# Outer products, key sums and query products moved from GpSimd to VectorE, batch 1 started behind chunk 0, scratch reads spread over 16 source rows

## The chip, the cores and the metric

The kernel runs on one NeuronCore of a Trainium2 chip. The metric is the device time of one launch in microseconds, as the median of several runs. The engines are named as the profile names them: PE (TensorE, matmuls), DVE (VectorE), ACT (ScalarE), POOL (GpSimd) and SP (SyncE, which here only issues transfers). Each has its own instruction stream, which it works through in program order; they meet at semaphores.

## What is computed

Two stages, everything in float32. First an attention with a polynomial feature map: every row of q and k (4 batches, 4 heads, 1088 rows of 32) is projected by two 8x32 matrices, and the outer product of the two projections gives 64 features. Then a gated feed-forward block runs over the 4352 tokens of 128 values which the attention gives.

```python
def phi(x):
    a = np.einsum('rd,bhsd->bhsr', S1, x)
    b = np.einsum('rd,bhsd->bhsr', S2, x)
    return np.einsum('bhsi,bhsj->bhsij', a, b).reshape(*x.shape[:-1], r * r)
q_p, k_p = (phi(q), phi(k))
kv = np.einsum('bhsf,bhsd->bhfd', k_p, v)
z = np.sum(k_p, axis=2)
num = np.einsum('bhsf,bhfd->bhsd', q_p, kv)
den = np.einsum('bhsf,bhf->bhs', q_p, z)[..., None] + 1e-06
x = (num / den)                       # then (B,H,S,D) -> (B*S, H*D)
gate = 1.0 / (1.0 + np.exp(-(x @ w_gate)))
out = (gate * (x @ w_val)) @ w_out    # 128 -> 1536 -> 128
```

## The kernel before

The feed-forward block is the bulk of the work. The tokens are cut into chunks of 512 (the ninth has 256). For each chunk the 1536 hidden units are worked through in twelve pieces of 128. One such piece is called a wave here: `w1` computes gate and value on PE into a two-bank PSUM tile `wave` (two buffers), ACT makes the sigmoid `sg`, DVE multiplies it with the value into `g` (`glu`, L317), and `w2` multiplies `g` with a slice of `w_out` on PE and accumulates into `moeout` (L256). `glu` of a wave is issued just before `w1` of the next one, and `w2` follows with a lag of two waves, so that PE has something to do while ACT and DVE work. After twelve waves DVE transposes the sum (`o_sb`, L266) and SP stores it.

The order of all instructions on PE, DVE, ACT and POOL is written out by hand: no scheduler moves them. The function `slot(group, waves)` issues one attention step (`group`) and then so many waves; the main program is a list of slots. A wave is only issued when its chunk's tokens exist (`moe["ready"]`).

The weights arrive in a 64-bit form and are narrowed on the chip while chunk 0 runs: `narrow` is a generator of four steps, whose operations are on POOL (`cap` L97, `head` L114), ACT (`tail` L101, `cap` L113) and DVE (`head` L105 and L109, `w_sb` L117). During chunk 0 each wave carries one round of them.

The attention of one batch goes through these steps:

- `turn_k` (L362), `turn_q` (L373): DVE transposes the loaded rows in blocks of 32. `turn_q` takes q in two parts, 8 and 9 blocks wide (`q_chk`); everything about q comes in these two parts, n = 0 and n = 1.
- `begin(b)`: `kps` (L385) projects k on PE, DVE transposes the result to `kab` (L395). `qcomp` (L474) projects q, ACT copies it to `cq`. `spread` (L498, L506) writes `cq` to a scratch in DRAM (`dq`) and reads it back in two arrangements, `qp` and `bq`, so that each of 64 features' two factors is in the right partition. Then `outer` forms the outer products of k, `kp` (L406).
- `sum_z` (L560 to L565): sums `kp` over nine row groups into `zs`.
- `kv` (L526, L538): the product of key features and values, and of the summed features and ones, on PE; ACT copies it to `kvd`.
- `ndt` (L571): PE transposes that; DVE and ACT copy it (`zb`, `nd`).
- `qmult(b, n)` (L515): `qp` times `bq`, the query features.
- `den(b, n)` (L591) and the `invert` that it returns (L602 to L609): the denominator on PE, and its reciprocal on DVE in four operations (`dT`, two on `rc`, `rb`).
- `num(b, n)` (L626) and its `divide` (L636): the numerator on PE and the division on DVE into `xT`, the token matrix.

For batch 0 the outer products are on DVE, and the first query part goes another way (`ab`). Its second part (`q01`) goes through the scratch like the other batches, and `qmult(0, 1)` is on DVE. For batches 1 to 3 `outer`, `sum_z` and `qmult` are on POOL. The main program before reads:

```python
slot(q01, 4)
turn_k(1)
slot(None, 2)
turn_q(1, 0)
turn_q(1, 1)
slot(None, 1)
qmult(0, 1, nc.vector)
slot(lambda: den(0, 1)(), 1)
slot(lambda: num(0, 1)(), 1)
```

and then a loop over batches 1 to 3, in which `turn_k` and `turn_q` of the next batch stand at the end.

Of the kernel before, what the change touches and what calls it, by code (L numbers as in the profile page):

```python
# [8 lines left out]
F32 = mybir.dt.float32  # L9
# [3 lines left out]
ALU = mybir.AluOpType  # L13
ACTF = mybir.ActivationFunctionType
MUL = ALU.mult

P = 128
# [3 lines left out]
def kernel(  # L21
# [12 lines left out]
    nc = tc.nc  # L34

    B, H, S, D = q.shape
    R = S1.shape[0]
    F = R * R
# [7 lines left out]
    NJK = 9  # L46
# [7 lines left out]
    sbA = ctx.enter_context(tc.tile_pool(name="sbA", bufs=2))  # L54
# [302 lines left out]
    def turn_k(b, t0=0, t1=T):  # L357
        if b >= B:
            return
        if t0 == 0:  # L360
            kT_of[b] = sbA.tile([P, T, 32], F32, tag="kT", name="kT", bufs=1)
        nc.vector.transpose(  # L362
            out=kT_of[b][:, t0:t1].rearrange("p t s -> p (t s)"),
            in_=k_t[b][:, t0:t1].rearrange("p t d -> p (t d)"),
        )

    def turn_q(b, n):
        if b >= B:
# [4 lines left out]
        nc.vector.transpose(  # L373
            out=qT_of[b][:, t0 : t0 + tn].rearrange("p t c s -> p (t c s)"),
            in_=q_t[b][:, 2 * t0 : 2 * (t0 + tn)].rearrange("p t d -> p (t d)"),
        )

    KP, QP, BQ, ND, KAB, ASB, KVZ, KVD, RB = {}, {}, {}, {}, {}, {}, {}, {}, {}

    def kps(b):  # L380
        t = ps2.tile([P, 2, 512], F32, tag="two", name="kps")
# [16 lines left out]
        KP[b] = sbA.tile([P, 2, NJK, 2, F], F32, tag="kp", name="kp")  # L398


    def outer(b, pi, m0, m1, j0=0, j1=NJK, eng=nc.gpsimd):
        a0 = KAB[b][:, pi, j0:j1, 2 * R * m0 :]
        pst = list(a0.ap[0])
        jm = [[2 * R, 2 * (j1 - j0)]] if m1 - m0 == 2 else [[4 * R, j1 - j0]]
        o0 = KP[b][:, pi, j0:j1, m0:m1]
        eng.tensor_tensor(  # L406
            out=o0.rearrange("p j m (i l) -> p (j m) i l", i=R),
            in0=bass.AP(tensor=a0.tensor, offset=a0.offset, ap=[pst] + jm + [[1, R], [0, R]]),
            in1=bass.AP(tensor=a0.tensor, offset=a0.offset + R, ap=[pst] + jm + [[0, R], [1, R]]),
            op=MUL,  # L410
        )
# [80 lines left out]
    def spread(b, ns, cq, eng=nc.sync):  # L492
        for n in ns:
            w = 32 * q_chk[n][1]
            d = dram.tile([2, 2, R, H, w], F32, tag=f"dq{n}", name="dq")
            for c in range(2):
                g = 2 * n + c
                eng.dma_start(  # L498
                    out=d[c].rearrange("i r (m p) w -> (i r m) p w", m=2),
                    in_=cq[32 * g : 32 * g + 32, :, :w],  # L500
                )
            for i, t in enumerate((QP[b], BQ[b])):
                for c in range(2):
                    d0 = d[c, i]
                    rows = [[H * w, R], [0, R]] if i == 0 else [[0, R], [H * w, R]]
                    nc.sync.dma_start(  # L506
                        out=half(t, n)[64 * c : 64 * c + 64].rearrange("p h w -> p (h w)"),
                        in_=bass.AP(
                            tensor=d0.tensor, offset=d0.offset, ap=rows + [[1, H * w]]
                        ),  # L510
                    )

    def qmult(b, n, eng=nc.gpsimd):
        q0 = half(QP[b], n)
        eng.tensor_tensor(out=q0, in0=q0, in1=half(BQ[b], n), op=MUL)  # L515

    def kv(b, j_list, zsum=None):

# [34 lines left out]
            ),  # L553
        )

    def sum_z(b):

        kp = KP[b].rearrange("p c j m f -> p c j (m f)")
        z4 = sbA.tile([P, 2, 4, 2 * F], F32, tag="z4", name="z4", bufs=1)
        nc.gpsimd.tensor_tensor(out=z4, in0=kp[:, :, 1:5], in1=kp[:, :, 5:9], op=ALU.add)  # L560
        nc.gpsimd.tensor_tensor(out=z4[:, :, :2], in0=z4[:, :, :2], in1=z4[:, :, 2:], op=ALU.add)
        zs = sbA.tile([P, H, F], F32, tag="zs", name="zs")
        zc = zs.rearrange("p (c m) f -> p c (m f)", c=2)
        nc.gpsimd.tensor_tensor(out=zc, in0=z4[:, :, 0], in1=z4[:, :, 1], op=ALU.add)
        nc.gpsimd.tensor_tensor(out=zc[:64], in0=zc[:64], in1=kp[:64, :, 0], op=ALU.add)  # L565
        return zs

    def ndt(b, pool=(ps1, "one")):
        ndps = pool[0].tile([P, 2, 256], F32, tag=pool[1], name="ndps")
# [77 lines left out]
    for _ in range(3):  # L647
# [9 lines left out]
        out=sk,  # L657
# [4 lines left out]
        op=MUL,  # L662
# [19 lines left out]
    mult10 = ab(None, (0, 1, 0), (psm, "wave"))  # L682
    for j0, j1 in ((0, 5), (5, NJK)):
        for pi in range(2):
            outer(0, pi, 0, 2, j0, j1, nc.vector)
        if j0 == 0:
            kv(0, [1, 2, 3, 4])
    narrow_w(0, 0)
# [21 lines left out]
    cq = {}  # L710

    def begin(b):
        glu()
        kps(b)
        cq[b] = qcomp(b, (0, 1), (psm, "wave"))
        spread(b, (0, 1), cq[b])
        for pi in range(2):
            for m in range(2):
                outer(b, pi, m, m + 1)

    def num0_den1(b):
        divide = num(b, 0)
        invert = den(b, 1)
        divide()
        invert()
# [65 lines left out]
```

## Time and profile before

| what | value |
|---|---|
| time, median of 3 runs | 314.44 us (313.09 to 315.10) |
| profiled execution | 318.37 us, span 316.6 us |
| PE busy | 302.6 us, 96% of the span |
| DVE busy | 137.0 us, 43% |
| ACT busy | 80.7 us, 25% |
| POOL busy | 66.0 us, 21% |
| DMA moved | 22.91 MB, 72 GB/s over the span |
| one wave on PE, L296 and L256 | 1.72 + 0.86 us |
| POOL: `outer` 14.0, `qmult` 14.9, `sum_z` L560 7.2 | us busy in all |

The busy shares tell which engine is full, not what a change is worth. PE is busy nearly all the time, so the time that can be won lies in those few places where it isn't, or where it runs slowly. These are found in the chain of work that ended last (its pieces in order of time show holes between PE's pieces), in the waits of PE, and in the timeline around each hole. The profiled execution is a little longer than the timed ones.

### The profile page before, as it was taken

What the parts mean: (1) busy time and instruction counts of PE and PEld (TensorE: products, weight loads), DVE (VectorE), ACT (ScalarE), POOL (GpSimd) and SP (SyncE); (2) the same over time, 40 slices, a digit from 0 to 9 for tenths busy, and PEclk for the clock granted to TensorE, in tenths of its full rate; (3) what the DMA queues carried; (4) which work ended last, traced back from release to release, by engine and by line L of the source; (5) the groups of instructions that cost most, each with busy time, mean ns of one, the idle gap of its engine ahead of it and who ended that gap; (6) DMA issues with size and microseconds to landing.
All of it is one profiled execution on the core that took longest, in us unless ns stands there. A gap on an engine that the chain in (4) does not pass through costs nothing.

```text
span 316.6 us, 3687 instructions
## 1 busy us (share of the span) xinstructions
PE 302.6 (96%) x1394; PEld 136.4 (43%) x1394; DVE 137.0 (43%) x235; ACT 80.7 (25%) x149; POOL 66.0 (21%) x64
## 2 busy tenths in 40 slices
PE   7889969999799999999999999999999999999995
PEld 2423313454234444443344444443444444444684
DVE  4988986323665221354453213552223223222321
ACT  2535513212113222222122222122222222222230
POOL 1346613951101942100019321000000000000000
PEclk9999968999999999999999999999999999999999
DMA  7996620455204456120005550020002000200021
GB/s 182 351 371 175 175 96 1 114 141 128 46 0 143 111 138 143 36 33 0 2 1 129 124 100 0 1 35 0 0 0 33 0 2 0 33 0 0 0 35 17
DMA packets 28465, 22.91 MB, mean 72 GB/s; under 512 B 19616, under 2 KB 23584, under 8 KB 28448
## 3 DMA queue, kind: packets, MB, share of 16 engines
q1 hardware_dynamic: 27520, 22.14, 27.0%
q10 hardware_dynamic: 928, 0.54, 0.8%
q8 instruction: 11, 0.18, 0.2%
q14 instruction: 6, 0.05, 0.1%
HBM read 19.46 MB, written 3.21 MB: 72 GB/s over the span
## 4 chain that ended last, share of the span: by engine, by line
PE 85%; DVE 8%; DMA 3%; issue 1%; POOL 1%; SPq 0%; ACT 0%; POOLq 0%; DVEq 0%
PE wave L296 52%; PE moeout L256 27%; DMA w_in<-in_moe_w_out_dram 2%; PE dps L591 2%; DMA k<-in_k_dram 1%; DVE w_sb L117 1%; PE nps L626 1%; PE kvz L526 1%; DVE head L105 1%; DVE g L317 1%; DVE rc L604 1%; DVE qp L515 1%; POOL head L114 1%; PE kps L385 1%; DVE head L109 1%
## 5 line engine op out<-in xcount | busy, mean ns | idle before, releaser
L296 PE MATMUL wave<-xT,w_sb 128*128 128x512 f32 (+1 forms) x432 | 192.6, 573 | 1.2 <-DVE w_sb L117 1.2
L317 DVE TENSOR_TENSOR g<-wave,sg 128x512 f32<-128x512 f32 x102 | 70.0, 688 | 143.0 <-ACT sg L304 142.7
L296 PEld LDWEIGHTS wave<-xT,w_sb 128*128 128x128 f32 x432 | 82.2, 191 | 97.2 <-issue 87.6
L304 ACT ACTIVATE sg<-wave 128x512 f32<-128x512 f32 x102 | 60.9, 597 | 212.1 <-PE wave L296 211.2
L256 PE MATMUL moeout<-g,w_sb 128*128 128x512 f32 (+1 forms) x216 | 105.5, 582 | 1.8 <-DVE g L317 1.8
L256 PEld LDWEIGHTS moeout<-g,w_sb 128*128 128x128 f32 x216 | 39.3, 191 | 46.3 <-issue 39.2
L406 POOL TENSOR_TENSOR kp<-kab 128x576 f32<-128x576 f32 x12 | 14.0, 1201 | 60.0 <-DVE kab L395 60.0
L515 POOL TENSOR_TENSOR qp<-qp,bq 128x1024 f32<-128x1024 f32 (+1 forms) x6 | 14.9, 2483 | 31.6 <-DMA bq<-dq 31.6
L114 POOL TENSOR_TENSOR head<-head,tail 128x384 int32<-128x384 int32 (+1 forms) x13 | 13.7, 1054 | 24.3 <-DVE head L109 22.9
L636 DVE TENSOR_TENSOR xT<-nps,rb 128x512 f32<-128x512 f32 (+1 forms) x8 | 5.8, 725 | 14.1 <-PE nps L626 14.0
L591 PE MATMUL dps<-qp,zb 128*32 128x256 f32 (+1 forms) x64 | 5.8, 438 | 3.3 <-DVE qp L515 3.1
L117 DVE SCALAR_TENSOR_TENSOR w_sb<-cap,head 128x384 f32<-128x384 f32 x12 | 8.1, 676 | 0.8 <-POOL head L114 0.8
L97 POOL TENSOR_SCALAR cap<-w_in 128x384 f32<-128x384 f32 x12 | 7.1, 594 | 5.0 <-DMA w_in<-in_moe_w_out_dram 5.0
L109 DVE SCALAR_TENSOR_TENSOR head<-cap,head 128x384 int32<-128x384 int32 (+1 forms) x13 | 7.6, 582 | 0.4
L113 ACT ACTIVATE cap<-cap 128x384 f32<-128x384 f32 (+1 forms) x13 | 6.5, 497 | 4.4 <-DVE head L109 4.4
L229 PE MATMUL warm<-ones 128*128 128x512 f32 (+1 forms) x10 | 6.6, 788 | 1.0 <-DVE hm L235 1.0
L560 POOL TENSOR_TENSOR z<-kp 128x1024 f32<-128x1024 f32 x3 | 7.2, 2406 | 0.2
L101 ACT ACTIVATE tail<-w_in 128x384 int32<-128x384 uint32 x12 | 6.6, 560 | 1.4 <-DMA w_in<-in_moe_w_out_dram 1.4
L626 PE MATMUL nps<-qp,nd 64*32 64x256 f32 (+1 forms) x128 | 6.1, 401 | 0.9 <-issue 0.9
L526 PEld LDWEIGHTS kvz<-kp,v 128*32 128x32 f32 (+1 forms) x288 | 5.3, 109 | 3.3 <-issue 2.7
L266 DVE STREAM_TRANSPOSE o_sb<-moeout 128x512 f32<-128x512 f32 (+1 forms) x9 | 6.1, 679 | 1.4 <-PE moeout L256 1.3
L526 PE MATMUL kvz<-kp,v 128*32 128x64 f32 (+1 forms) x288 | 6.6, 222 | 0.1
(57 smaller groups left out, 88.5 us busy)
## 6 DMA issues: line engine op xcount, KB each, us to landing
v<-in_v_dram SPq DMA_DIRECT2D x16, 144.0 KB
qp<-dq SPq DMA_DIRECT2D x8, 288.0 KB
bq<-dq SPq DMA_DIRECT2D x8, 288.0 KB
k<-in_k_dram SPq DMA_DIRECT2D x3, 544.0 KB
q<-in_q_dram SPq DMA_DIRECT2D x3, 544.0 KB
w_in<-in_moe_w_gate_dram SPq DMA_DIRECT2D x6, 256.0 KB
w_in<-in_moe_w_val_dram SPq DMA_DIRECT2D x6, 256.0 KB
w_in<-in_moe_w_out_dram SPq DMA_DIRECT2D x6, 256.0 KB
```

Source lines behind the costliest of these rows:

```text
L109: nc.vector.scalar_tensor_tensor(out=head, in0=cap, scalar=-0x40000000, in1=head, op0=ALU.bitwise_and, op1=ALU.bitwise_or)
L114: nc.gpsimd.tensor_tensor(out=head, in0=head, in1=tail, op=ALU.add)
L117: nc.vector.scalar_tensor_tensor(out=out, in0=cap.bitcast(F32), scalar=1.265625 * 2.0**-30, in1=head.bitcast(F32), op0=ALU.is_ge, op1=MUL,)
L256: nc.tensor.matmul(out=moe["acc"][:, :tw], lhsT=w_sb[:, 2, j, :], rhs=g[:, jj, :tw], start=(j == 0), stop=(j == NJ - 1),)
L296: nc.tensor.matmul(out=wv[:, which, jj * tw : (jj + 1) * tw], lhsT=w_sb[:, which, j0 + jj, :], rhs=xT[:, t0 : t0 + tw], start=True, stop=True,
L304: nc.scalar.activation(out=sg, in_=wv[:, 0], func=ACTF.Sigmoid)
L317: nc.vector.tensor_tensor(out=g, in0=wv[:, 1], in1=sg, op=MUL)
L406: eng.tensor_tensor(out=o0.rearrange("p j m (i l) -> p (j m) i l", i=R), in0=bass.AP(tensor=a0.tensor, offset=a0.offset, ap=[pst] + jm + [ ...
L515: eng.tensor_tensor(out=q0, in0=q0, in1=half(BQ[b], n), op=MUL)
L526: nc.tensor.matmul(out=kvz[32 * h : 32 * h + 32, F * which : F * which + F], lhsT=v_t[b][:kr, h, j, :] if which == 0 else ones[:kr, :], rh ...
L591: nc.tensor.matmul(out=dps[32 * h : 32 * h + 32, :w], lhsT=zb[b % 2][:, h, :], rhs=half(QP[b], n)[:, 2 * (h % 2) + h // 2, :], start=True, ...
L626: nc.tensor.matmul(out=nps[32 * h : 32 * h + 32, c, :w], lhsT=ND[b][rows, 32 * h : 32 * h + 32], rhs=half(QP[b], n)[rows, 2 * (h % 2) + h ...
```

## The change

Four edits, made together:

1. `outer`, `sum_z` and `qmult` of batches 1 to 3 go from POOL to DVE. `outer` takes both head pairs' halves at once (two operations of 128x1152 for a batch in place of four of 128x576). `sum_z` is cut into two steps, and each piece is put between waves.
2. Batch 1 moves behind chunk 0: its `turn_k` and `turn_q` no longer stand between the waves of chunk 0, `slot(q01, 8)` runs eight waves without them, and each batch is turned at the start of its own round.
3. `spread` writes `cq` in pieces of 16 partitions, four for each part in place of two, with the scratch laid out so that the reading of `qp` is one transfer whose source has 16 rows, each read 8 times, in place of two transfers whose sources have 8 rows each. The reading of `bq` stays two transfers of 8 repeats.
4. The loop over batches has another list of slots: one wave (batch 1) or two waves (batches 2 and 3) after each attention step.

It is meant [...] to bring the second query part of batch 0 forward, and to use more of the transfer engines for the scratch.

```diff
-    def outer(b, pi, m0, m1, j0=0, j1=NJK, eng=nc.gpsimd):
+    def outer(b, pi, j0=0, j1=NJK):
...
-        eng.tensor_tensor(
-            out=o0.rearrange("p j m (i l) -> p (j m) i l", i=R),
...
+        nc.vector.tensor_tensor(
+            out=KP[b][:, pi, j0:j1].rearrange("p j m (i l) -> p (j m) i l", i=R),
...
             for c in range(2):
-                g = 2 * n + c
-                eng.dma_start(
-                    out=d[c].rearrange("i r (m p) w -> (i r m) p w", m=2),
-                    in_=cq[32 * g : 32 * g + 32, :, :w],
+                for i in range(2):
+                    p0 = 64 * n + 32 * c + 16 * i
+                    eng.dma_start(
+                        out=d[i, c].rearrange("r (m p) w -> (r m) p w", m=2),
+                        in_=cq[p0 : p0 + 16, :, :w],
+                    )
+
+            nc.sync.dma_start(
+                out=half(QP[b], n).rearrange("p h w -> p (h w)"),
+                in_=bass.AP(
+                    tensor=d.tensor, offset=d.offset, ap=[[H * w, 2 * R], [0, R], [1, H * w]]
+                ),
+            )
...
-    def qmult(b, n, eng=nc.gpsimd):
+    def qmult(b, n):
         q0 = half(QP[b], n)
-        eng.tensor_tensor(out=q0, in0=q0, in1=half(BQ[b], n), op=MUL)
+        nc.vector.tensor_tensor(out=q0, in0=q0, in1=half(BQ[b], n), op=MUL)
...
-    def sum_z(b):
-
+    def sum_z(b, step):
...
+        def add(out, in0, in1):
+            nc.vector.tensor_tensor(out=out, in0=in0, in1=in1, op=ALU.add)
...
-        for pi in range(2):
-            for m in range(2):
-                outer(b, pi, m, m + 1)
...
-    slot(q01, 4)
-    turn_k(1)
-    slot(None, 2)
-    turn_q(1, 0)
-    turn_q(1, 1)
-    slot(None, 1)
-    qmult(0, 1, nc.vector)
+    slot(q01, 8)
+    qmult(0, 1)
     slot(lambda: den(0, 1)(), 1)
     slot(lambda: num(0, 1)(), 1)
     for b in range(1, B):
         more = b + 1 < B
-        wn = 2 if b == 1 else 3
+        wn = 1 if b == 1 else 2
+        turn_k(b)
+        turn_q(b, 0)
+        slot(None, wn)
+        turn_q(b, 1)
+        slot(lambda: begin(b), 1)
         load_kq(b + 1)
-        slot(lambda: begin(b), wn)
-        zs = sum_z(b)
-        slot(None, 2 * wn - 1)
-        qmult(b, 0)
-        slot(lambda: kv(b, [1, 2, 3, 4, 5, 6, 7, 8, 0], zs), wn)
+        for pi in range(2):
+            outer(b, pi)
+            slot(None, wn)
+        for step in range(2):
+            sum_z(b, step)
+            slot(None, wn)
+        slot(lambda: kv(b, [1, 2, 3, 4, 5, 6, 7, 8, 0], ZS[b]), wn)
         if more:
             v_t[b + 1] = load_v(b + 1)
-        slot(lambda: ndt(b), wn - 1)
+        slot(lambda: ndt(b), wn)
+        qmult(b, 0)
+        slot(lambda: den(b, 0)(), wn)
         qmult(b, 1)
-        slot(lambda: den(b, 0)(), wn)
-        slot(lambda: num0_den1(b), wn)
-        slot(lambda: num(b, 1)(), 1)
-        turn_k(b + 1)
-        slot(None, 1)
-        turn_q(b + 1, 0)
-        turn_q(b + 1, 1)
-        slot(None, 1)
+        slot(lambda: num0_den1(b), wn + 1)
+        slot(lambda: num(b, 1)(), 3)
     slot(None, 10**3)
```

More of the change, by code (lines that the diff above doesn't have):

```diff
@@ L376, in turn_q @@
         )
-    KP, QP, BQ, ND, KAB, ASB, KVZ, KVD, RB = {}, {}, {}, {}, {}, {}, {}, {}, {}
+    KP, QP, BQ, ND, KAB, ASB, KVZ, KVD, RB, Z4, ZS = ({} for _ in range(11))
     def kps(b):
@@ L398, in kps @@
         KP[b] = sbA.tile([P, 2, NJK, 2, F], F32, tag="kp", name="kp")
[L401 to L409 removed]
+    def outer(b, pi, j0=0, j1=NJK):
+        a0 = KAB[b][:, pi, j0:j1]
+        ap = [list(a0.ap[0]), [2 * R, 2 * (j1 - j0)]]
+        nc.vector.tensor_tensor(
+            out=KP[b][:, pi, j0:j1].rearrange("p j m (i l) -> p (j m) i l", i=R),
+            in0=bass.AP(tensor=a0.tensor, offset=a0.offset, ap=ap + [[1, R], [0, R]]),
+            in1=bass.AP(tensor=a0.tensor, offset=a0.offset + R, ap=ap + [[0, R], [1, R]]),
             op=MUL,
@@ L496, in spread @@
             for c in range(2):
-                g = 2 * n + c
-                eng.dma_start(
-                    out=d[c].rearrange("i r (m p) w -> (i r m) p w", m=2),
-                    in_=cq[32 * g : 32 * g + 32, :, :w],
-                )
[L502 to L511, printed above, removed]
-    def qmult(b, n, eng=nc.gpsimd):
+                for i in range(2):
[10 more added lines that the diff above has]
+            )
+            for c in range(2):
+                d0 = d[1, c]
+                nc.sync.dma_start(
+                    out=half(BQ[b], n)[64 * c : 64 * c + 64].rearrange("p h w -> p (h w)"),
+                    in_=bass.AP(
+                        tensor=d0.tensor, offset=d0.offset, ap=[[0, R], [H * w, R], [1, H * w]]
+                    ),
+                )
+    def qmult(b, n):
         q0 = half(QP[b], n)
-        eng.tensor_tensor(out=q0, in0=q0, in1=half(BQ[b], n), op=MUL)
+        nc.vector.tensor_tensor(out=q0, in0=q0, in1=half(BQ[b], n), op=MUL)
     def kv(b, j_list, zsum=None):
@@ L554, in kv @@
         )
-    def sum_z(b):
+    def sum_z(b, step):
         kp = KP[b].rearrange("p c j m f -> p c j (m f)")
[L559 to L566, printed above, removed]
+        def add(out, in0, in1):
+            nc.vector.tensor_tensor(out=out, in0=in0, in1=in1, op=ALU.add)
+        if step == 0:
+            Z4[b] = sbA.tile([P, 2, 4, 2 * F], F32, tag="z4", name="z4", bufs=1)
+            add(Z4[b], kp[:, :, 1:5], kp[:, :, 5:9])
+            return
+        z4 = Z4[b]
+        add(z4[:, :, :2], z4[:, :, :2], z4[:, :, 2:])
+        ZS[b] = sbA.tile([P, H, F], F32, tag="zs", name="zs", bufs=1)
+        zc = ZS[b].rearrange("p (c m) f -> p c (m f)", c=2)
+        add(zc, z4[:, :, 0], z4[:, :, 1])
+        add(zc[:64], zc[:64], kp[:64, :, 0])
     def ndt(b, pool=(ps1, "one")):
@@ L684 @@
         for pi in range(2):
-            outer(0, pi, 0, 2, j0, j1, nc.vector)
+            outer(0, pi, j0, j1)
         if j0 == 0:
```

## The prediction

> **What bounds the kernel now.** I read the busy shares first, then the slices, then PE's waits, then the timeline around the two largest waits, and last the granted clock there.
>
> ```profile
> PE 302.6 (96%) x1394; PEld 136.4 (43%) x1394; DVE 137.0 (43%) x235; ACT 80.7 (25%) x149; POOL 66.0 (21%) x64
> ...
> PE   7889969999799999999999999999999999999995
> ...
> POOL 1346613951101942100019321000000000000000
> PEclk9999968999999999999999999999999999999999
> ```
>
> PE is full. From slice 12 (95 us) on it shows no hole at all, so whatever DVE or POOL do in batches 2 and 3 costs nothing today. The weak slices are the start, slices 5 and 6 (40 to 55 us, low clock with them) and slice 10 (79 to 87 us).
>
> ```profile
> PE dps L591 <- DVE qp L515: 3.1, 1, 3.1
> PE moeout L256 <- DVE g L317: 1.8, 1, 1.8
> PE wave L296 <- DVE w_sb L117: 1.2, 3, 0.6
> ```
>
> PE's waits are few: two single ones and a sum of 1.2 us in chunk 0. The timeline names what made them. First the one at 40 to 43 us:
>
> ```profile
> 37.90 0.60 ACT L304 ACTIVATE sg<-wave 128x512 f32<-128x512 f32 x1 [1.65 <-PE wave L296]
> 38.05 1.36 DVE L373 STREAM_TRANSPOSE qT<-q 128x512 f32<-128x512 f32 x2
> ...
> 39.34 0.65 DVE L317 TENSOR_TENSOR g<-wave,sg 128x512 f32<-128x512 f32 x1
> ...
> 41.02 1.15 POOL L114 TENSOR_TENSOR head<-head,tail 128x384 int32<-128x384 int32 x1 [1.51 <-DVE head L109]
> 41.23 2.15 DVE L515 TENSOR_TENSOR qp<-qp,bq 128x1152 f32<-128x1152 f32 x1
> ...
> 43.44 1.19 PE L591 MATMUL dps<-qp,zb 128*32 128x288 f32 x8 [3.06 <-DVE qp L515]
> ```
>
> `qmult(0, 1)` is late because DVE first does `turn_q(1)`, then the gate product, then three narrowing operations, then itself, at 2.15 us. Next the one at 80 to 82 us:
>
> ```profile
> 77.92 2.62 POOL L515 TENSOR_TENSOR qp<-qp,bq 128x1152 f32<-128x1152 f32 x1 [6.78 <-DMA bq<-dq]
> ...
> 78.18 2.38 DVE L604 TENSOR_SCALAR rc<-dT 128x16 f32<-128x16 f32 x1
> ...
> 82.23 1.12 PE L256 MATMUL moeout<-g,w_sb 128*128 128x512 f32 x2 [1.83 <-DVE g L317]
> ```
>
> The 16-element operation on `rc` took 2.38 us; its 18-element sister takes 0.17 (172 ns mean). It ended at 80.56, and POOL's product ended at 80.54. DVE stood still, the gate products behind it came late, PE waited 1.83 us. The clock during the first wait (columns: stretch, sum, busy of PE, PEld, DVE, ACT, POOL, then clock, DMA share, GB/s):
>
> ```profile
> 41.00:42.00 1.00, 0.00 (x0) 0.00 (x0) 1.00 (x2) 0.93 (x3) 0.98 (x1) 1.00 0.97 379
> 42.00:43.00 1.00, 0.00 (x0) 0.00 (x0) 1.00 (x1) 0.00 (x0) 0.16 (x1) 0.77 0.16 60
> 43.00:44.00 1.00, 0.56 (x8) 0.20 (x8) 0.38 (x1) 0.00 (x0) 0.00 (x0) 0.50 0.00 0
> ...
> 49.00:50.00 1.00, 1.00 (x15) 0.18 (x16) 0.00 (x0) 0.13 (x1) 0.25 (x1) 0.82 0.00 0
> ...
> 81.00:82.00 1.00, 0.00 (x0) 0.00 (x0) 1.00 (x2) 0.10 (x1) 0.00 (x0) 1.00 0.00 0
> ```
>
> After the 3.06 us wait PE runs at half clock from about 42.5 to 49.4 us; after the 1.83 us wait it doesn't slow. The half clock cost some 2.7 us: the denominator took 1.19 for 0.7, the next `moeout` 2.07 for 1.02, the wave 3.34 for 1.88, less what pipelining hides.
>
> [...] The half-clock stretch here is 6.9 us[...]. [...] Here POOL takes 1201 ns for 576 elements, DVE 798 for 640. [...] The trace shows share 0.52 at 131 GB/s in the scratch reads (61 to 64 us), against 0.97 at 379 GB/s in a load.
>
> **Part by part.**
>
> *POOL's work to DVE.* DVE prices: 798 ns for 640 elements and 685 for 512 (`outer` of batch 0), about 1 ns per element more. That gives 1.3 us for 1152 elements, 1.2 for 1024, 0.7 for 512, and 0.4 each for the last two sums. For a batch: two `outer` 2.6, sums 1.2 + 0.7 + 0.4 + 0.4 = 2.7, `qmult` 1.2 + 1.3, in all 7.8 us, or 23.4 for three batches. DVE would be at 160 of 312 us. POOL loses 44 us, and is empty after chunk 0. What hides DVE's part: around 108 us DVE idles 2.74 us before a gate product, waiting for `sg`; and that product (109.93 to 110.62) is wanted by the `moeout` at 111.7, 1.1 us later. So a piece of up to 2.7 us between two gate products costs PE nothing, and the largest new piece is 1.4 (or `kab` and `outer`, 2.1). Batches 2 and 3: 0. Batch 1 loses its lock wait: -1.83, and -0.26 for the restart (1.12 in place of 0.86).
>
> *`qmult` on DVE as a wait in the queue.* It now waits for a transfer with gate products queued behind it, for which PE waits. In batch 1 part 0 stands about 18 us after the copy of `cq`, part 1 about 23 us. Before, the parts landed 13.5 us (68.7 against 55.2) and 22.6 us (77.85) after it. [...] As part 1's writes now stand behind part 0's reads in SP's order, I give 2 us back: landing at about 20 us, 3 before it is wanted. Cost 0, bound 3.
>
> *Batch 1's transposes out of chunk 0.* Without `turn_q` ahead, the gate product starts when `sg` ends (38.50 in place of 39.34). The rest is as before: gate and narrowing 1.97, product 2.07 with POOL's `head` in its way. So `dps` starts some 4.7 us after the last but one wave's end, wanted at 2.5: a wait of 2.2 us (bounds 1.4 with no lock, 2.7 if narrowing runs as at 30 us, where it took 2.43). That is -0.8. `turn_k` at 32.56 pushed a wave from 35.4 to 36.0; -0.5. The turns now stand behind narrowing and before `begin(1)`: there the second query part may come 0.3 us late for `qcomp`, +0.2.
>
> *Four writes on ACT in place of two* in `q01`: ACT issued two in 0.82 us, so the sigmoid behind them is 0.8 later; through gate product and narrowing that reaches a wave which had 0.37 us of room (`w_sb` ended 27.30, wave at 27.67): +0.4 once.
>
> *Waves.* The same 102 waves and the same attention matmuls, at 1.72 + 0.86 us: 0.
>
> Sum: -1.83 - 0.26 - 0.8 - 0.5 + 0.4 + 0.2 = -2.8. 314.44 - 2.8 = 311.6 us. This takes the half-clock stretch as unchanged.
>
> **Rivals.**
>
> A, the clock stays full[...]. For it: the 1.83 us wait left the clock alone. [...] It gives another 2.7: 308.9 us.
>
> B, slower: DVE becomes the place where PE waits. Eight new pieces in each of three batches; if each holds PE for 0.3 us, since it begins just before `sg` is ready, that is 7.2, and a `qmult` that waits for its transfer adds up to 3. For it: DVE is in strict order, and batch 1 has one wave a piece. Against: the room of 2.7 and 1.1 us above. 311.6 + 7.2 = 318.8.
>
> C, no change: the lock wait at 78 us is a coincidence of landing time and denominator, which the timed runs needn't have, and the wait before `dps` stays. Only 0.9 is left: 313.5. Against it: such a coincidence has a width of 2.6 us, the length of POOL's product.
>
> **How the numbers follow.** Forecast (310.4 to 312.8) 0.43; A (308 to 310.3) 0.27; B (315 to 320) 0.20; C (312.8 to 315) 0.10. Faster by over 1% is below 311.3: all of A and just under half of the forecast, 0.48. Slower by over 1% is above 317.6: three quarters of B, 0.15. The rest, 0.37, is within 1%. The range 308.2 to 316.0 leaves out most of B and the edge of A.
>
> **What would show it.** After: POOL without any L404, L519 or L565 work, and idle from about 55 us; no operation on `rc` above 0.3 us; no wait of PE on a gate product above 0.5 us; one wait of `dps` on `qp` of about 2.2 us; DVE near 160 us busy; the scratch reads at a DMA share above 0.6. Half clock after the wait decides between the forecast and A. Wrong would be: PE waits repeated in each batch, DVE waiting for `bq`, or a wait before `dps` as long as before.

## The result, and the profile after

Measured together, the changed kernel took 317.43 us (median of 4 runs, 317.06 to 318.14) against 314.03 us (313.09 to 315.10) of the kernel before: a ratio of 1.011, 95% interval 1.0069 to 1.015. A second, longer comparison gave 318.07 us (22 runs) against 315.55 (68 runs), 1.0079 (1.0056 to 1.0103). The change made the kernel slower by about 1%. (Ratios leave out runs over 1.5% above the fastest of their kernel; medians and ranges here and below keep them.) 311.6 us had been predicted, and the range ended at 316.0.

First the page of the kernel after, with the rows that answer to those shown of before.

```profile
PE 301.3 (95%) x1394; PEld 136.1 (43%) x1394; DVE 156.8 (50%) x259; ACT 80.7 (26%) x149; POOL 21.7 (7%) x34
...
PE   7888969999899999999999999999999999999994
...
POOL 1346631000000000000000000000000000000000
PEclk9999988999999999999999999999999999999999
```

The work did move: GpSimd is idle from the eighth slice (55 us) on, and VectorE has 20 us more. The rows of the new VectorE work cost what was foreseen (the mean of L519 has batch 0's product of 2.16 us in it, from 43.87 us on, beside which GpSimd's `head` runs from 43.65 to 44.80; the other three take 1.35):

```profile
L404 DVE TENSOR_TENSOR kp<-kab 128x1152 f32<-128x1152 f32 x6 | 8.0, 1327 | 0.0
L519 DVE TENSOR_TENSOR qp<-qp,bq 128x1152 f32<-128x1152 f32 x4 | 6.2, 1554 | 0.5 <-DMA bq<-dq 0.5
L565 DVE TENSOR_TENSOR z<-kp 128x1024 f32<-128x1024 f32 x3 | 3.6, 1216 | 0.0
```

Now PE's waits after (total, times, longest). Three are waits for a query product before the denominator `dps`, though two of them name the instruction that came last by the profile, and not the product.

```profile
PE dps L601 <- DVE qp L519: 2.6, 1, 2.6
PE wave L296 <- DVE w_sb L117: 1.2, 3, 0.6
...
PE dps L601 <- ACT sg L304: 0.9, 1, 0.9
PE dps L601 <- PE nps L636: 0.9, 1, 0.9
```

The wait of 1.8 us on a gate product is gone, and the one at 40 us went from 3.06 to 2.63. Two waits of 0.9 are new.

**Where the time went, by a ledger.** Every wave begins with one sigmoid (L304), so the starts of the 102 sigmoids date all the work. I compare the kernel after with a second trace of the kernel before (the first experiment), since the trace of before on record turned out to be untypical. Both were at half clock for one stretch of 3.41 us in chunk 0.

| from wave to wave | before, second trace | after | difference |
|---|---|---|---|
| start to 0 | 20.22 | 20.81 | +0.59 |
| 0 to 3 (the scratch writes on ACT) | 9.03 | 9.78 | +0.75 |
| 3 to 13 (rest of chunk 0, `qmult(0, 1)`) | 33.85 | 32.92 | -0.93 |
| 13 to 24 (batch 1) | 33.30 | 34.27 | +0.97 |
| 24 to 71 (batches 2 and 3) | 133.63 | 134.99 | +1.36 |
| 71 to 101 | 76.46 | 76.47 | 0 |

The sum is +2.75 us. The first row isn't the change's: sigmoid 0 starts between 19.84 and 20.81 in the traces of kernels that are alike up to there. Without it 2.15 us are left.

### The profile page after: what moved, and what is told of

The parts are those of the page before. It is cut to its first block, busy times and chain, and to the rows that moved or that the text cites. A ratio compares the mean times of both kernels' runs of the same rounds, so it can differ in the third digit from the quotient of the medians.

```text
span 316.0 us, 3673 instructions
## 1 busy us (share of the span) xinstructions
PE 301.3 (95%) x1394; PEld 136.1 (43%) x1394; DVE 156.8 (50%) x259; ACT 80.7 (26%) x149; POOL 21.7 (7%) x34
## 4 chain that ended last, share of the span: by engine, by line
PE 87%; DVE 4%; DMA 4%; issue 1%; ACT 1%; POOL 1%; SPq 0%; ACTq 0%; POOLq 0%; DVEq 0%
PE wave L296 53%; PE moeout L256 28%; DMA w_in<-in_moe_w_out_dram 2%; PE dps L601 2%; DMA k<-in_k_dram 2%; PE nps L636 1%; PE kvz L530 1%; DVE w_sb L117 1%; ACT sg L304 1%; DVE qp L519 1%; DVE g L317 1%; POOL head L114 1%; DVE head L105 1%; DVE head L109 1%; DMA dq<-cq 1%
## 5 line engine op out<-in xcount | busy, mean ns | idle before, releaser
L304 ACT ACTIVATE sg<-wave 128x512 f32<-128x512 f32 x102 | 60.9, 597 | 210.4 <-PE wave L296 206.4
L404 DVE TENSOR_TENSOR kp<-kab 128x1152 f32<-128x1152 f32 (+2 forms) x10 | 10.7, 1092 | 0.0
L519 DVE TENSOR_TENSOR qp<-qp,bq 128x1152 f32<-128x1152 f32 (+1 forms) x7 | 9.9, 1409 | 0.5 <-DMA bq<-dq 0.5
L117 DVE SCALAR_TENSOR_TENSOR w_sb<-cap,head 128x384 f32<-128x384 f32 x12 | 7.3, 608 | 0.8 <-POOL head L114 0.8
L105 DVE TENSOR_SCALAR head<-cap 128x384 int32<-128x384 int32 (+1 forms) x13 | 6.4, 495 | 0.6 <-POOL cap L97 0.5
```

The source lines that it names most:

```text
L105: nc.vector.tensor_scalar(out=head, in0=cap, scalar1=3, scalar2=0x3FFFFFF8, op0=ALU.logical_shift_left, op1=ALU.bitwise_and,)
L117: nc.vector.scalar_tensor_tensor(out=out, in0=cap.bitcast(F32), scalar=1.265625 * 2.0**-30, in1=head.bitcast(F32), op0=ALU.is_ge, op1=MUL,)
L304: nc.scalar.activation(out=sg, in_=wv[:, 0], func=ACTF.Sigmoid)
L404: nc.vector.tensor_tensor(out=KP[b][:, pi, j0:j1].rearrange("p j m (i l) -> p (j m) i l", i=R), in0=bass.AP(tensor=a0.tensor, offset=a0.of ...
L519: nc.vector.tensor_tensor(out=q0, in0=q0, in1=half(BQ[b], n), op=MUL)
```

## The experiments

**1. The kernel before once more, and the kernel after once more** (no edit).

> The kernel before, unchanged, to get a second trace of it. Theory 1 (the trace that the prediction was read from was not typical): the span is 311 to 313 us, and at least one of the two large waits in it is missing or smaller: POOL's product no longer meets the 16-element operation on rc (1.83 us), or the wait before dps leaves the clock full [...]. Theory 2 (that trace was typical, and the changed kernel loses elsewhere): span near 316, both waits there. Time by both: equal to before, ratio 1.00.

> The changed kernel, unchanged, beside more runs of the kernel before than the first time. Theory 1 (the losses seen in its trace come in every run, while the large waits in the first trace of before come in few) expects a ratio of 1.005 to 1.011 and a span of 314.5 to 316. If the first comparison was chance, the ratio is within 0.997 to 1.003.

Before: 315.24 us, ratio to before 0.9993 (0.9961 to 1.0025); its trace is of a run of 314.49 us. In the trace on record GpSimd's product in batch 1 began 0.26 us ahead of the operation on `rc`, which took 2.38 us in place of 0.17 and ended 0.02 us after the product. This hold on `rc` is what the prediction counts as the lock wait. The two operations in the second trace:

```profile
76.43 0.17 DVE L604 TENSOR_SCALAR rc<-dT 128x16 f32<-128x16 f32 x1
76.64 0.25 DVE L605 RECIPROCAL rc<-rc 128x16 f32<-128x16 f32 x1
76.95 2.62 POOL L515 TENSOR_TENSOR qp<-qp,bq 128x1152 f32<-128x1152 f32 x1 [7.42 <-DMA bq<-dq]
```

The transfer landed half a microsecond after DVE had passed. No hold on `rc` (0.17 us), no PE wait on a gate product, and nothing there for the change to gain. The half clock lasted 3.41 us there, not 6.83. The trace that the prediction was read from (318.37 us) was 4 us above the median mainly for these two reasons: by the ledger it took 2.10 us more in waves 13 to 24, and 1.42 more in waves 3 to 13.

The times of before say how usual each is (229 runs, on which the ratios of four comparisons rest). The granted clock of a run gives its time at half clock as 2 x (1 - clock) x span, an estimate, since the clock is listed to three digits. The runs at full clock have a median of 313.75 us (55 runs, up to 0.6 us at half clock), those with about 3.4 us (3.1 to 4.4) at half clock 315.38 (137), those with about 6.8 us 316.46 (29). Inside the first two classes the times have two groups: 10 of 55 lie above 314.5, 30 of 137 above 316.2, some 2 us above the others: about one in five of these runs.

The kernel after is 2.8 to 2.9 us slower in each class (316.55 at full clock, 6 runs; 318.31 with about 3.4 us at half clock, 13 runs), so its loss doesn't come from the clock.

**2. Edit 3 alone in the kernel before** (four writes a part, 16 source rows), and three more traces of the same kernel.

```diff
-            for c in range(2):
-                g = 2 * n + c
-                eng.dma_start(
+                for i in range(2):
+                    p0 = 64 * n + 32 * c + 16 * i
+                    eng.dma_start(
...
```

> The kernel before with edit 3 alone (four scratch writes a part, 16 source rows for qp). Theory 1 (the four writes hold ScalarE's queue, and the sigmoid behind them, for some 2 us; the wait before dps is set by VectorE's order and gains nothing): waves 0 to 3 take 0.7 us longer than the 9.0 of before, wait 3 us as before, ratio 1.002 to 1.004. By the prediction's price: +0.4, ratio 1.001. Rival (the better-spread reading lands earlier and pays it back): ratio 0.998.

> The kernel before with edit 3 alone, once more, for its trace. Theory 1: where the time, less half of the us at half clock, lies some 2 us above the other trace of this kernel, an operation on rc of batch 1 takes over 1 us, because GpSimd's query product runs at that moment. Rival: the time is that high with every operation on rc at 0.17 us, and the 2 us lie elsewhere.

318.06 us, ratio 1.0103 (1.0071 to 1.0136): alone, this edit costs as much as the whole change, and more than the ratio of 1.002 to 1.004 expected. Its own trace is of the fastest of its 19 runs. A part is seen in ACT's row. First the second trace of before, then the kernel after, each from the writes to the sigmoid behind them:

```profile
23.24 0.82 ACTq L498 DMA_DIRECT2D dq<-cq  x2
24.11 0.60 ACT L304 ACTIVATE sg<-wave 128x512 f32<-128x512 f32 x1 [0.90 <-ACT cq L486]
```

```profile
23.83 1.99 ACTq L497 DMA_DIRECT2D dq<-cq  x4
25.87 0.60 ACT L304 ACTIVATE sg<-wave 128x512 f32<-128x512 f32 x1 [2.06 <-DMA dq<-cq]
```

The sigmoid stands behind all writes in ACT's queue, and starts 0.05 us after the last of them in both. How long the issue took varied from trace to trace: two writes 0.82 to 2.17 us, four 1.76 to 2.95. In each trace all writes but one took 0.35 to 0.44 us, and one, mostly the second, 0.43 to 1.78. Two of the longest, two writes (old `spread` of experiment 3) and four (second trace of the kernel after), with count, then shortest, median and longest in ns:

```profile
L496 ACTq DMA_DIRECT2D dq<-cq x2: 347/1064/1782, 23.7 to 24.0; - x2
L497 ACTq DMA_DIRECT2D dq<-cq x4: 347/432/1617, 23.2 to 25.7; - x4
```

So the two further writes cost 0.86 us of issue, and the rest is a swing that kernels with two writes have too. Waves 0 to 3 took 9.03 and 9.10 us with an issue of 0.82 and 1.31, then 9.55, 9.78, 9.96, 10.74 with 1.76, 1.99, 2.17, 2.95. From about 1.3 us on every further 0.1 us of issue is 0.1 us of time.

The other part: of three more traces of this kernel two show the hold on `rc`, and one just misses it. First the longest, then the miss:

```profile
75.53 2.62 POOL L521 TENSOR_TENSOR qp<-qp,bq 128x1152 f32<-128x1152 f32 x1 [7.49 <-DMA bq<-dq]
75.92 2.26 DVE L610 TENSOR_SCALAR rc<-dT 128x16 f32<-128x16 f32 x1
...
79.84 1.12 PE L256 MATMUL moeout<-g,w_sb 128*128 128x512 f32 x2 [1.70 <-DVE g L317]
```

```profile
77.36 0.18 DVE L610 TENSOR_SCALAR rc<-dT 128x16 f32<-128x16 f32 x1
77.42 2.62 POOL L521 TENSOR_TENSOR qp<-qp,bq 128x1152 f32<-128x1152 f32 x1 [7.71 <-DMA bq<-dq]
```

In the second trace GpSimd started 0.06 us after the operation on `rc`, which took its usual 0.18. Of nine traces of kernels with GpSimd's product in batch 1, three have it start first, by 0.26 to 0.90 us, and there the operation on `rc` ended 0.02 to 0.03 us after the product; in the other six it started 0.06 to 0.72 us later. GpSimd's product took 2.62 us in both traces above.

From wave 18 to 19 the three traces took 4.48, 2.52 and 3.97 us: the hold on `rc` costs 1.5 to 2.0 us when it comes, as theory 1 had it, and that is about the distance of the two groups of times. That the hold makes the upper group of before in every run isn't shown, since only traced runs tell. The clock may be a third part: each of the 19 runs was at half clock for 3.1 us or more, and 59 of the 229 of before for no more than 1.9. How the cost of this edit divides among the three stays open.

**3. Edit 3 taken out of the kernel after (the `spread` of before in it, whole), and, in another run, only its writes on ACT given to SyncE:**

```diff
-    spread(0, (1,), qcomp(0, (1,), (ps2, "two")), nc.scalar)
+    spread(0, (1,), qcomp(0, (1,), (ps2, "two")))
```

> The changed kernel with the old spread: two writes of 32 partitions, reads with 8 source rows. Theory 1 holds that the four writes on ACT's queue hold the sigmoid of the second wave for 2.06 us and cost PE about 1 us, so this is 0.5 to 1 us faster than the changed kernel (316.4 to 317). The rival (the 16 source rows pay, since the products of batch 1 wait for their transfers less) expects qmult(1, 1) to wait about 4 us instead of 0.48 and the time to be 2 to 3 us longer (319 to 320).

> The changed kernel with the four scratch writes of batch 0 issued by SP in place of ACT. If ACT's wait for transfers in flight is the cost, the sigmoid of the second wave starts at once, no wave of chunk 0 waits more than 0.7 us, and it is 1 us faster (316.4). If it costs nothing on the path (the wait before dps takes it up), the time is the same as the changed kernel, 317.4.

With the old `spread`: 317.44 us, 1.0053 (1.0026 to 1.008). With the writes on SyncE: 316.18 us, 1.0026 (1.0003 to 1.0049). In that trace waves 0 to 3 take 9.10 us, and nothing else in the ledger gets worse; so the writes on ACT are some 0.7 to 1.6 us of the loss (9.78 and 10.74 in the two traces of the kernel after). The old `spread` brings the issue on ACT no reliable gain (2.17 us for two writes in its trace), and in batch 1 it is worse: waves 13 to 24 take 34.98, as the transfer lands 1.19 us after VectorE was ready for it, in place of 0.48. The new layout does its work in batch 1, and its two further writes cost at the start; over the whole kernel the two can't be told apart (1.0053 and 1.0079, with intervals that overlap), so neither what theory 1 nor what the rival expected came.

**4. Edit 1 alone in the kernel before**: `outer`, `sum_z`, `qmult` on VectorE where they stood.

```diff
-    def outer(b, pi, m0, m1, j0=0, j1=NJK, eng=nc.gpsimd):
+    def outer(b, pi, m0, m1, j0=0, j1=NJK, eng=nc.vector):
...
```

> The kernel before with edit 1 alone: outer, sum_z and qmult of batches 1 to 3 on VectorE at the places where they stood, so in blocks of about 3 us (outer) and 2.7 (sum_z). By the prediction's steps it gains the lock wait of 2.1 us and pays nothing: 312.3, ratio 0.993. Theory 1 (in a usual run there is no lock wait to gain, and a product that waits for its transfer, or a block longer than the room of 2.7 us, holds PE): 316 to 318.5, ratio 1.003 to 1.01, with new waits of PE on gate products in batch 1.

317.78 us, 1.006 (1.0034 to 1.0086). Uncut, the pieces hold PE: the narrowing of a weight slice stands behind four `outer` in a row, and the wave behind that.

```profile
54.16 2.72 DVE L406 TENSOR_TENSOR kp<-kab 128x576 f32<-128x576 f32 x4
56.80 0.55 DVE L117 SCALAR_TENSOR_TENSOR w_sb<-cap,head 128x384 f32<-128x384 f32 x1
57.27 0.68 DVE L317 TENSOR_TENSOR g<-wave,sg 128x512 f32<-128x512 f32 x1
57.50 1.53 PE L296 MATMUL wave<-xT,w_sb 128*128 128x512 f32 x3 [0.67 <-DVE w_sb L117]
```

Against the second trace of before it loses 0.90 us at wave 11, 0.31 at wave 19, 0.50 at wave 51, and no more than 0.11 elsewhere from wave 3 on. So it was right to cut the pieces as the change does; what the change loses is elsewhere.

**5. The query products of batches 1 to 3 back on GpSimd, in the kernel after.**

```diff
-        nc.vector.tensor_tensor(out=q0, in0=q0, in1=half(BQ[b], n), op=MUL)
+        (nc.gpsimd if b else nc.vector).tensor_tensor(out=q0, in0=q0, in1=half(BQ[b], n), op=MUL)
```

> The changed kernel with qmult of batches 1 to 3 back on POOL, in the same places. Theory (the losses in batches 1 and 3, 0.97 and 1.36 us against the second trace of before, are qmult standing between a gate product and dps in DVE's order): dps of batch 3 no longer waits 0.94 us and that of batch 1 not 0.91, and the time is 1 to 2 us shorter than the changed kernel, unless POOL's slower product (2.4 to 2.6 us) is itself late for dps. Rival (outer and sum_z on DVE delay the gate products): no change in time, the same waits.

317.48 us, 1.0048 (1.0026 to 1.007). The wait of 0.9 in batch 3 goes, but in batch 1 `dps` now waits 2.45 us for the slower product, since this part lands at 80.7 us and the denominator stands right behind. So the place of the product matters on either engine.

**6. One wave between a query product and the denominator that reads it** (kernel after).

```diff
         qmult(b, 0)
+        if b > 1:
+            slot(None, 1)
         slot(lambda: den(b, 0)(), wn)
         qmult(b, 1)
+        slot(None, 1)
         slot(lambda: num0_den1(b), wn + 1)
-        slot(lambda: num(b, 1)(), 3)
+        slot(lambda: num(b, 1)(), 2 if b == 1 else 1)
```

> The kernel after, with one wave between a query product on VectorE and the denominator that reads it: for part 1 of all three batches, and for part 0 of batches 2 and 3. The last slot of each batch gives the waves back. Theory 1 (the product stands directly in front of a reader, with nothing on PE to cover its wait or its 1.2 to 1.4 us): the wait of 0.9 us before dps in batch 3 and the one of 0.9 to 1.2 in batch 1 go, the interval of waves 13 to 24 falls by about 0.9 us and that of waves 62 to 63 by 0.9; span near 314.1, ratio to before 1.002. Rival (the loss of batches 1 and 3 lies in the outer products and sums on VectorE): the waits reappear on gate products, ratio 1.006 or more.

316.01 us (14 runs), ratio 1.0006 (0.9976 to 1.0036), from 1.0079 without it. Batch 1 in the kernel after, then with the wave between:

```profile
81.56 0.66 PE L636 MATMUL nps<-qp,nd 64*32 64x256 f32 x16
81.67 1.36 DVE L519 TENSOR_TENSOR qp<-qp,bq 128x1152 f32<-128x1152 f32 x1 [0.48 <-DMA bq<-dq]
...
83.13 0.69 PE L601 MATMUL dps<-qp,zb 128*32 128x288 f32 x8 [0.91 <-PE nps L636]
```

```profile
79.18 1.36 DVE L519 TENSOR_TENSOR qp<-qp,bq 128x1152 f32<-128x1152 f32 x1 [0.21 <-DMA bq<-dq]
...
80.10 1.88 PE L296 MATMUL wave<-xT,w_sb 128*128 128x512 f32 x4
...
82.50 0.69 PE L601 MATMUL dps<-qp,zb 128*32 128x288 f32 x8
```

In the first, PE has nothing between the numerator and `dps`, and the 1.36 us of the product lie bare. In the second a wave lies over them. Waves 13 to 24 take 33.30 us, as in before; waves 24 to 71 take 133.99 (after 134.99, before 133.63). So 1.97 of the 2.33 us that batches 1 to 3 lost are explained by the place of the product. Most of the other 0.36 shows as a wait that no trace of the kernel before has: behind the projections of batch 3's `begin`, where a chunk ends, a wave waits 0.28 us for a gate product and then takes 1.99 us in place of 1.88. It is there with the query products on GpSimd too (experiment 5). In the kernel after:

```profile
169.84 1.99 PE L296 MATMUL wave<-xT,w_sb 128*128 128x512 f32 x4 [0.28 <-DVE g L317]
```

Both kernels are the same in chunk 0, and had the same wait there, but only the kernel after went to half clock. The stretches around it, of the kernel after and then of the one with the wave between (columns as before):

```profile
43.00:44.00 1.00, 0.45 (x2) 0.00 (x0) 1.00 (x3) 0.45 (x1) 0.35 (x1) 1.00 0.00 0
44.00:45.00 1.00, 0.00 (x0) 0.00 (x0) 1.00 (x1) 0.56 (x2) 0.80 (x1) 1.00 0.00 0
45.00:46.00 1.00, 0.00 (x0) 0.00 (x0) 1.00 (x1) 0.00 (x0) 0.00 (x0) 0.88 0.00 0
46.00:47.00 1.00, 0.92 (x8) 0.20 (x8) 0.02 (x1) 0.00 (x0) 0.00 (x0) 0.50 0.00 0
```

```profile
43.00:44.00 1.00, 0.00 (x0) 0.00 (x0) 1.00 (x2) 0.80 (x2) 1.00 (x1) 1.00 0.00 0
44.00:45.00 1.00, 0.00 (x0) 0.00 (x0) 1.00 (x1) 0.00 (x0) 0.04 (x1) 1.00 0.00 0
45.00:46.00 1.00, 0.69 (x9) 0.23 (x9) 0.25 (x1) 0.00 (x0) 0.00 (x0) 1.00 0.00 0
```

PE stood still for 2.63 us in one and 2.6 in the other; behind it the clock was half for 3.41 us in the first, and stayed full here in the second. So two waits that differ by 0.03 us went either way, and what decides between them isn't shown. That a wait of 2.2 us could leave the clock full, as rival A had it, was the author's estimate.

**7. The wait in chunk 0 itself**: the product of batch 0's second part two waves earlier in the kernel after; ahead of `turn_q` and one wave earlier in the kernel before; and in before, two matmuls (128x512, result unused) that fill the wait. The three edits:

```diff
-    slot(q01, 8)
+    slot(q01, 6)
     qmult(0, 1)
+    slot(None, 2)
```

```diff
     turn_k(1)
     slot(None, 2)
-    turn_q(1, 0)
-    turn_q(1, 1)
-    slot(None, 1)
     qmult(0, 1, nc.vector)
+    slot(None, 1)
     slot(lambda: den(0, 1)(), 1)
+    turn_q(1, 0)
     slot(lambda: num(0, 1)(), 1)
+    turn_q(1, 1)
```

```diff
     qmult(0, 1, nc.vector)
+    fill = ps2.tile([P, 2, 512], F32, tag="two", name="fill")
+    for which in range(2):
+        nc.tensor.matmul(
+            out=fill[:, which, :], lhsT=w_sb[:, 0, 0, :], rhs=xT[:, :512], start=True, stop=True
+        )
     slot(lambda: den(0, 1)(), 1)
```

> The changed kernel with qmult(0, 1) two waves earlier, so that dps finds its operand ready. If the wait before dps (2.63 us) and the half clock behind it (about 2 us) are on the path, this is 3 to 4.5 us faster than the changed kernel (313 to 314.4), with no half clock after 40 us; the product itself may cost 0.5 us of PE in chunk 0, where DVE is full. If PE's wait were taken up elsewhere (narrowing of the weights as the real limit of chunk 0), under 1 us.

> The kernel before with qmult(0, 1) one wave earlier and the two parts of turn_q(1) after den(0, 1): everything else, POOL too, as before. If the wait before dps (3.05 us) and the half clock behind it are what can be won in chunk 0, the wait is under 0.5 us, no half clock follows, and it is 3 to 4.5 us faster than before (ratio 0.986 to 0.990), with less spread. If narrowing on DVE is the limit of chunk 0 and takes the wait up, under 1 us.

> The kernel before with two more matmuls of 128x512 on PE (0.86 us each, their result unused) queued ahead of dps of batch 0, where PE waits 3.05 us anyway. They leave 1.3 us of idle time, so the clock should stay full: that separates the half clock from the wait. Theory: no half clock at 43 us, the wait before dps about 1.3 us, time 1.5 to 2.7 us shorter than before. Rival (the half clock costs nothing, since DVE's chain sets the pace there): equal to before.

After, early: 315.41 us, 1.0003 (0.9978 to 1.0028), times from 314.74 to 316.08 only; by the ratios that is 2.4 us below the kernel after, less than the 3 to 4.5 expected. Before, early: 314.01 us, 0.996 (0.9939 to 0.9981); `dps` still waits 2.3 us, because the product then stands ready before its transfer does:

```profile
41.15 1.36 DVE L515 TENSOR_TENSOR qp<-qp,bq 128x1152 f32<-128x1152 f32 x1 [3.18 <-DMA bq<-dq]
```

Before, filled: 313.51 us, 0.9944 (0.9919 to 0.9969). The wait is 1.3 us, and none of its 15 runs was at half clock for more than 1.2 us; of before, 170 of the 229 runs were for 3.1 us or more. With the product early it is 4 of 21. The two matmuls only fill the wait, and that is worth 1.8 us: the filled kernel is within 0.3 us of before's own runs at full clock (313.75).

**8. Three repairs together**: in the kernel after the wave between, the writes on SyncE and the early product; in the kernel before the `spread` of edit 3, the writes on SyncE and the early product (edits as shown above).

> The kernel after with three repairs together: the wave between as in the run beside it (-1.9 us), the four scratch writes of the first batch's second part issued by SyncE instead of ScalarE (-0.9), and its query product two waves earlier (no wait of 2.6 before dps, no half clock: -2.6). Theory 1, all three losses are separate: 317.9 - 5.4 = 312.5 us, ratio 0.991. Rival: the second and third repair act on the same stretch, and the early product then makes gate products late: about 315, ratio 0.999.

> The kernel before with the new scratch layout (16 source rows for qp), its second query part written by SyncE, and its product before turn_q with a wave between product and denominator. Theory 1 (with the product early, the landing of bq at 41.1 us was what dps still waited 2.3 us for): landing comes before 40 us, the wait falls below 1 us and the half clock goes: 312.5 to 313.5 us, ratio 0.991 to 0.994. Rival (landing doesn't move with the source rows, since bq still has 8 of them): wait 2 us, ratio 0.996.

After: 315.77 us, 1.0016 (0.9991 to 1.0041). Before: 317.18 us, 1.0033 (1.0009 to 1.0057). Theory 1 fell in both: the repairs don't add up. In the kernel after it went as the rival said, with late gate products; the kernel before came out slower than either theory had it. Before, with them:

```profile
41.70 1.36 DVE L521 TENSOR_TENSOR qp<-qp,bq 128x1152 f32<-128x1152 f32 x1 [3.93 <-DMA bq<-dq]
...
43.11 1.19 PE L597 MATMUL dps<-qp,zb 128*32 128x288 f32 x8 [3.08 <-DVE qp L521]
```

Written by SyncE, the part lands at 41.7 us in the kernel before and at 40.6 in the kernel after; written by ACT, it landed at 41.15 in the kernel before with the old layout (experiment 7), and in the kernel after the early product of the next experiment starts at 38.58 without any wait for a transfer. An early product that waits for its transfer holds the gate products behind it: in the repaired kernel after, PE waits 2.7 us for `g` in place of `qp`. The repaired kernel before still has its query products on GpSimd and the new layout, as in experiment 2: four of its 22 runs lie below 315.4 us, the others above 316.5. Its trace is of one of the four (315.27) and has no hold on `rc`; that the others have one is likely, but no trace shows it.

**9. Two repairs in the kernel after, with the writes left on ACT** (the wave between, and the early product), and in another run the wave between with the two matmuls in front of `den(0, 1)` (edits as shown above).

> The kernel after with the wave between query product and denominator, and the query product of batch 0's second part two waves earlier; the scratch writes stay on ScalarE. Theory 1 (two separate losses; with the writes on SyncE the landing came later, at 40.6 us, and took the second gain away): no wait of dps on qp above 0.7, no half clock, 313.5 us, ratio 0.993. Rival (both repairs act on one loss): 315.5, ratio 1.000.

> The kernel after with the wave between, and two extra matmuls of 128x512 (result unused) in front of the denominator of batch 0's second part. If the half clock comes in a part of the runs and costs 1.5 to 2 us each time, cutting the idle time of 2.6 us to 1.7 takes it away at no cost, since the two matmuls fill idle time: no clock below 0.9 in the trace, ratio 0.995 to 0.998. Rival (the half clock is rare in timed runs): ratio 1.000 to 1.002.

Two repairs: 313.23 us (312.91 to 313.88, 22 runs) against 315.33, ratio 0.9942 (0.9925 to 0.9958). It is faster than both kernels, as the filled kernel before is (0.9944); the two have the same ratio within their intervals. Theory 1 held. In chunk 0:

```profile
38.58 2.16 DVE L519 TENSOR_TENSOR qp<-qp,bq 128x1152 f32<-128x1152 f32 x1
...
41.39 1.13 PE L256 MATMUL moeout<-g,w_sb 128*128 128x512 f32 x2 [0.55 <-DVE g L317]
...
44.64 0.69 PE L601 MATMUL dps<-qp,zb 128*32 128x288 f32 x8
```

The wait before `dps` is gone, for 0.55 and 0.9 us on gate products, and none of the 22 runs was at half clock for more than 2.5 us. With the two matmuls instead: 314.78 us, 0.9987 (0.997 to 1.0005), and no more than 2.5 us in 22 runs either; the ratio lies between the 0.995 to 0.998 of the theory and the 1.000 of the rival.

## Why the prediction was wrong

Two steps failed: the hold on `rc` (the lock wait), counted as 2.1 us gained in every run, and the query products on VectorE, put at no cost, which cost 2.0 us. The cost of the writes on ACT had the right sign and was about half of what it came to.

| step | predicted, us | measured, us | from |
|---|---|---|---|
| hold on `rc` (lock wait) and restart | -2.1 | 0 in a usual run | experiments 1 and 2 |
| wait before `dps`, transposes, `qT` | -0.8 - 0.5 + 0.2 = -1.1 | -0.93 | ledger, waves 3 to 13 |
| four writes on ACT | +0.4 | +0.75 (0.5 to 1.7) | ledger, experiments 2 and 3 |
| `qmult` on VectorE, batch 1 | 0, bound 3 | +0.97 | ledger, experiment 6 |
| other VectorE pieces, batches 2 and 3 | 0 | +1.36, of which 1.0 is `qmult` | experiment 6 |

The measured steps sum to +2.15 us, the predicted ones to -2.8; the longer comparison gave +2.5. Edits 2 and 4 were not run by themselves; what is said of their part rests on the ledger.

*The largest error was the hold on `rc`.* It was there in the trace (2.38 us in place of 0.17), and the change takes it away (the longest operation of its kind on `rc` is 0.175 us after). But the gain was read from one execution. The prediction had the thought as rival C, and argued that the coincidence was 2.6 us wide; it gave it 0.10. But what counted was the distance to its edge: in that trace the product began only 0.26 us ahead of the operation on `rc`, and over the nine traces its start moved from 0.90 us ahead to 0.72 behind. The hold is in about one run of five by the groups of times, so its mean worth was about 0.4 us (an estimate, 2 us in a fifth of the runs), and for the median nothing. That the traced run was 318.37 us, and the median 314.44, was on the page: 4 us that had to be somewhere in that trace. They were put down to profiled executions being a little longer; the second trace is of a run of 314.49 us, below the median of its 14 runs (315.24).

*"Landing at about 20 us, 3 before it is wanted. Cost 0"* failed twice. Part 1 of batch 1 was there at 81.67 us, 22.6 after the copy of `cq` had ended (59.04), just as long as in the trace of before. With 22.6 us before and 2 us given back, this takes the reading to be some 4 us shorter by its 16 source rows: an estimate of the author that no trace shows by itself. The 2 us were too few: SyncE issued three of the eight writes only behind part 0's reads, so that part 1's reads were issued 12.5 us after the copy (71.54), against 4.9 in the second trace of before (58.40 and 53.48).

```profile
62.09 0.62 SPq L510 DMA_DIRECT2D bq<-dq  x1
62.81 0.56 SPq L502 DMA_DIRECT2D qp<-dq  x1
63.46 0.60 SPq L510 DMA_DIRECT2D bq<-dq  x1
64.10 1.37 SPq L497 DMA_DIRECT2D dq<-cq  x3
71.54 0.60 SPq L510 DMA_DIRECT2D bq<-dq  x1
```

The second half is plainer, and would have cost time with any landing: the working asked what stands behind the product in VectorE's queue, the gate products with their room of 1.1 to 2.7 us, but not who reads the product. In the new list `den` stands right behind `qmult`. In batch 1 PE has only the numerator in between; in batch 3 the product comes at a chunk's boundary, where two waves run in a row (eight matmuls, 201.07 to 204.67 us) and `dps` stands directly behind them. Here the wait of 0.94 us is put down to a sigmoid, though what stands before it is the product, from 204.28 to 205.50:

```profile
203.67 0.69 DVE L317 TENSOR_TENSOR g<-wave,sg 128x512 f32<-128x512 f32 x1 [1.54 <-ACT sg L304]
204.28 1.22 DVE L519 TENSOR_TENSOR qp<-qp,bq 128x1024 f32<-128x1024 f32 x1
204.76 0.60 ACT L304 ACTIVATE sg<-wave 128x512 f32<-128x512 f32 x1 [1.12 <-PE wave L296]
205.60 0.64 PE L601 MATMUL dps<-qp,zb 128*32 128x256 f32 x8 [0.94 <-ACT sg L304]
```

*The ACT writes* had the right cause and the right room: 2 x 0.82 = 1.64 us of issue less 1.24 us of room (1.99 us of issue cost 0.75) is the predicted 0.4. What was mis-sized is the issue: 0.41 us a write is the price where nothing holds it, and in most traces one write took longer, up to 1.78 us.

*Right were* the prices on VectorE (156.8 us busy for 160 predicted, and pieces of up to 1.33 us between gate products at no cost: waves 24 to 46, all of batch 2, took 62.96 us in both kernels), the empty GpSimd, the end of the hold on `rc`, and the gain in chunk 0, though its parts differ: the wait fell by 0.43 instead of 0.8. Taking the half clock as unchanged was right too, since the loss is the same in each class. The foreseen DMA share above 0.6 holds for part 1's reads (0.66 at 72 to 76 us), but not for part 0's (0.49 at 62 to 66 us). Rival B named the right place, VectorE ahead of PE, but with the wrong cause: not 24 pieces at 0.3 us but two products at 1 us each.

## What to carry to other kernels

Before a wait of a trace is counted as a gain, hold the traced run against the median of the times and look at a second trace: a coincidence of a landing transfer with another engine's operation is worth its share of the runs, not its length. When work moves to another queue, ask for each piece both who stands behind it and who reads it next; keep one piece of PE's own work between a product and its reader. Repairs on one stretch are to be run together, since an earlier consumer finds the next limit, here the landing of the transfer.

## What the runs showed of the hardware

- The half clock lasted 3.41 us in the second trace of before and in the kernel after, and 6.83 in the trace of before on record. The runs of before fall into classes (medians 313.75, 315.38, 316.46 us) with none, about 3.4 and about 6.8 us of it. Behind a wait of 2.63 us it came in one trace, and behind one of 2.6 in another of the same code up to there it did not. Two filling matmuls, which cut a wait of 3.05 us to 1.3, narrowed the times from 312.9 to 320.1 us (the 68 runs of before beside them) down to 312.8 to 315.2 (15 runs).
- Issuing two small transfers from ACT's queue took from 0.82 to 2.17 us in kernels alike up to there, and the activation behind them waits all that time. One write took 0.35 to 0.44 us, but one of each group of writes up to 1.78. What held the issue isn't settled: the profile names an earlier transfer in some traces and nothing in others.
- The operation on `rc` that begins 0.06 us before GpSimd's product takes its usual 0.18 us; one that begins 0.39 us after it took 2.26, until the product had ended. Not every operation on VectorE is held: in the trace with the 0.06 us the reciprocal and the transpose that follow took 0.25 and 0.71 us while GpSimd's product ran, as long as in the second trace of before.
